# Eight groups' second product in plain float32, their weights split a block a slot later, and four units' row remainder on TensorE

## The chip, the cores and the metric

The kernel runs on one core of a Trainium2 chip. Its engines work side by side, each in its own order: TensorE (PE in the rows; PEld is its weight load), VectorE (DVE), ScalarE (ACT), GpSimd (POOL) and SyncE (SP), which issues the transfers. The metric is the device time in microseconds of one execution; lower is better.

## The reference

Three stages follow each other. The change touches the first two.

```python
for t in range(S):                        # S = 768, 4 batches, 8 heads of width 48
    cur = einsum('bhd,bhe->bhde', u * kt, vt)
    y[:, :, t] = einsum('bhd,bhde->bhe', rt, state + cur)
    state = wt[..., None] * state + einsum('bhd,bhe->bhde', kt, vt)
# x = y with the heads side by side: [4, 768, 384]
h = maximum(x @ w_in, 0)                  # w_in [384, 1024], float64
gate = 1 / (1 + exp(-conv3(h, conv_w)))   # three taps along the sequence
x2 = (h * gate) @ w_out                   # w_out [1024, 384], float64
# then causal attention with 4 experts of width 64, two chosen per row
```

The scan's inputs are float32; w_in, conv_w and w_out come as float64 and are made float32 on the chip.

## The kernel before

**Units and groups.** The scan is cut into 32 units u: a batch, a half of the sequence (384 steps) and a pair of heads. Units 0 to 3 are the four pairs of the first half of batch 0, units 4 to 7 of its second half, and so on. The middle stage is cut into 64 groups g = 8 bh + f: bh is a half of a batch, f one of eight blocks of 128 columns of w_in. A group is a product `hs` (`mlp1`, L434, nine matmuls), ReLU on ScalarE into `ht`, three taps (`conv_a`, `conv_b`, into `ct`), tanh (L471, into `st`) and the gate (`gate`, L480), and then the second product `x` with w_out (`mlp2`, L508), which adds over the eight f of a bh into three PSUM tiles.

**Three products for one.** A float32 matrix is held as a high part rounded to fp32r and a low part, the rest. A product takes high x high, low x high and high x low. For `x` that is nine matmuls a group: `high` (L487, ScalarE) and `low` (L495, VectorE) make the two parts of the gated rows, and the parts of w_out stand in two tiles `wout0` and `wout1`. The rows of the scan get their two parts in `rows`: ScalarE copies the rounded rows out of PSUM (L408), VectorE subtracts (L409), and two to four transfers bring both into X, the input of `hs` (L417).

**Weights.** `load_w` brings a block of w_in or w_out, four each, as float64. `conv0_w` and `conv1_w` make float32 of it by work on the bits (VectorE, ScalarE, GpSimd), `conv2_w` rounds it to the high part (L209, ScalarE), `conv3_w` subtracts (L214, VectorE). The table `WS` says in which slot a block begins; its conv2 and conv3 are one slot later, for w_out in slots 5, 7, 8 and 9.

**The order.** For TensorE, VectorE, ScalarE and GpSimd the order is the code's own: `slot(u)` is written out by hand, and each engine does its instructions in that order, waiting where an input or a buffer is not there. SyncE's order is the scheduler's. With ga = 2u - 11, slot u holds `hs` of groups ga and ga + 1, each followed by `x` of three groups earlier: group 0 is begun in slot 5, `x` of group 0 in slot 7, of group 7 in slot 10. Around them, on TensorE: `trans(u)` (L325), `es` for the early units (L330), `hs`, `x`, `scores` (L310), `state` (L343), `yout(u - 1)` (L388, L396), from slot 8 on `carried` (L359), `hs`, `x`. On VectorE: taps of the group before, `scan_d(u + 1)` (L249), `queries`, `gate`, `low`, `scan_f` (L257), taps, `keys` (L264), `low`, `gate`, the weights' conv3 and conv1, `masked` (L316), the row part of unit u - 1 (L409), from slot 8 on `carry2` (L372). On ScalarE the copies and tanh of the same steps, `scaled` (L353, `Ss`) among them; `trans` of the next slot needs the PSUM buffer that `scaled` reads. From slot 8 on, `carry2` sends the state through two transfers into Bd, which `yout` of the next slot reads.

Of the kernel before, what the change touches and what calls it, by code (L numbers as in the profile page):

```python
# [10 lines left out]
F32 = mybir.dt.float32  # L11
# [5 lines left out]
OP = mybir.AluOpType  # L17
# [33 lines left out]
def _f(ap):  # L51
    return ap.bitcast(F32)
# [52 lines left out]
def phase1(tc, nc, a, x2, ident, stat, lim, top, right, left2):  # L105
# [83 lines left out]
    win = [wt.tile([128, 4, 3, 256], F32R, name=f"win{i}") for i in range(2)]  # L189
    wout = [wt.tile([128, NF, DM], F32R, name=f"wout{i}") for i in range(2)]  # L190
    both = dict(win=win, wout=wout)
    wl = lambda t: t.rearrange("p a b c -> p (a b c)") if len(t.shape) == 4 else t.rearrange("p a b -> p (a b)")
# [9 lines left out]
    def conv1_w(n, i):  # L202

        if wide:
            RW[n, i] = f64_fast(nc, raw, RW[n, i], RW.pop((n, i, 0)), WC, "w")

    def conv2_w(n, i):

        nc.scalar.activation(wl(both[n][0])[:, i * WC:(i + 1) * WC], RW[n, i], AF.Copy)  # L209

    def conv3_w(n, i):
        t = RW.pop((n, i))
        d0, d1 = (wl(d)[:, i * WC:(i + 1) * WC] for d in both[n])
        nc.vector.tensor_tensor(d1, t, _f(d0), op=OP.subtract)  # L214

# [184 lines left out]
    def rows(u):  # L400
# [73 lines left out]
    def gate(g):  # L474
        if not 0 <= g < NG:
            return
        h = g // NF % 2
        o, N = 2 * h, HT - 2 + 4 * h
        ht, st = G[g]
        nc.vector.scalar_tensor_tensor(st, st, 1.0, ht[:, o:o + N], op0=OP.add, op1=OP.mult)  # L480
        G[g] = st

    def high(g):
        if not 0 <= g < NG:
            return
        gh = ml.tile([128, HT + 2], F32R, name="gh", bufs=LAG + 2)[:, 0:HT - 2 + 4 * (g // NF % 2)]
        nc.scalar.activation(gh, G[g], AF.Copy)  # L487
        G[g] = gh, G[g]

    def low(g):  # L490
        if not 0 <= g < NG:
# [8 lines left out]
    def mlp2(g):  # L500
# [3 lines left out]
        if f == 0:  # L504
            acc[0] = [ps_x.tile([128, HT + 2], F32, name=f"x{i}") for i in range(3)]
        for i in range(3):
            for z, (wi, gi) in enumerate(((0, 0), (1, 0), (0, 1))):
                nc.tensor.matmul(acc[0][i][:, 0:N], wout[wi][:, f, i * 128:(i + 1) * 128], G[g][gi],  # L508
                                 start=(f == 0 and z == 0), stop=(f == NF - 1 and z == 2))
# [25 lines left out]
    def slot(u):  # L535
# [741 lines left out]
```

## Time and profile before

| | us |
|---|---|
| median of 3 runs | 610.92 (610.88 to 611.37) |
| the profiled execution | 614.61 |
| its span, first to last instruction | 612.9 |
| TensorE busy in the span | 573.2 (94%) |
| VectorE busy | 493.8 (81%) |
| ScalarE busy | 400.0 (65%) |

Busy times of engines overlap, so they don't add up to the span. A busy share is a mean over stages of different limits; what a change in one stage is worth is read in that stage. Matmuls are pipelined: a matmul's own length is longer than its distance from the next, so their pace is read from start to start. A bracket at the end of a row in order of time gives the engine's idle time ahead of the row and who ended it. [...]

### The profile page before, as it was taken

The numbers are of one execution on the slowest core, as the hardware profiler recorded it, in microseconds if no ns is written. First come the engines' busy times: TensorE is split into PE (matmuls) and PEld (weight loads), VectorE is DVE, ScalarE is ACT, GpSimd is POOL, SyncE is SP. The second block draws the span as 40 slices with busy tenths as digits, with TensorE's granted clock in tenths as the row PEclk, the third lists the DMA queues.
The fourth block names the chain that finished last, engine by engine and source line by source line (L and its number), as shares of the span: only waits on it lengthen the run. The fifth ranks groups of instructions, "written<-read, shape, count | busy, mean of one in ns | idle before, by whom it ended". The sixth has DMA issues, their size and how long they took to land.

```text
span 612.9 us, 12380 instructions
## 1 busy us (share of the span) xinstructions
PE 573.2 (94%) x4374; PEld 514.4 (84%) x4374; DVE 493.8 (81%) x1139; ACT 400.0 (65%) x1013; POOL 188.6 (31%) x246
## 2 busy tenths in 40 slices
PE   4998988999999999999997999999979998999896
PEld 4887877999989999899997999797869887888754
DVE  6999999999999999999866955996748683876561
ACT  4886656777767888897765755865556555656542
POOL 3665563434524344242416300300030002004070
PEclk9999889999999999999999999999998999899999
DMA  8886445655656668776235425661265226422502
GB/s 283 279 268 186 144 137 139 184 144 143 206 159 184 180 218 297 216 219 164 73 83 160 141 52 151 172 156 40 65 180 136 60 78 167 111 67 72 141 2 83
DMA packets 46583, 91.00 MB, mean 148 GB/s; under 512 B 14256, under 2 KB 27824, under 8 KB 46512
## 3 DMA queue, kind: packets, MB, share of 16 engines
q1 hardware_dynamic: 46512, 90.12, 50.8%
q8 instruction: 37, 0.61, 0.4%
q14 instruction: 34, 0.28, 0.1%
HBM read 50.82 MB, written 9.44 MB: 98 GB/s over the span
## 4 chain that ended last, share of the span: by engine, by line
PE 59%; DVE 19%; ACT 8%; DMA 6%; issue 3%; POOL 2%; SPq 1%; ACTq 0%; DVEq 0%; POOLq 0%
PE hs L434 11%; PE x L508 10%; PE m L925 8%; PE st L999 6%; PE m L1049 6%; PE t L1033 5%; PE m L1061 4%; PE m L955 4%; DMA x<-x 3%; DVE Dp L249 3%; PE sc L310 2%; DVE ct L453 2%; DVE Fp L257 2%; PE m L396 2%; DVE ct L466 2%
## 5 line engine op out<-in xcount | busy, mean ns | idle before, releaser
L434 PE MATMUL hs<-X,win 128*128 128x384 f32 (+1 forms) x576 | 120.7, 355 | 4.5 <-ACT ht L438 4.4
L434 PEld LDWEIGHTS hs<-X,win 128*128 128x128 f32 x576 | 101.0, 193 | 8.1 <-ACT ht L438 5.8
L508 PE MATMUL x<-gh,wout 128*128 128x386 f32 (+1 forms) x384 | 99.2, 340 | 0.0
L293 POOL TENSOR_SCALAR_AFFINE_SELECT AT<-e 128x384 f32<-128x384 f32 x52 | 44.1, 869 | 125.3 <-DVE e L283 102.0
L1013 ACT ACTIVATE A<-sm,mn 128x128 f32<-128x128 f32 (+5 forms) x96 | 63.7, 664 | 23.2 <-DVE mn L1012 22.5
L1012 DVE CUSTOM_DVE_ANT_0 sm<-st,mask 128x128 f32<-128x128 f32 (+5 forms) x96 | 58.1, 616 | 20.5 <-PE st L999 19.0
L471 ACT ACTIVATE st<-ct 128x382 f32<-128x382 f32 (+1 forms) x64 | 33.6, 526 | 62.4 <-DVE ct L466 34.4
L508 PEld LDWEIGHTS x<-gh,wout 128*128 128x128 f32 x384 | 71.0, 191 | 0.0
L508 PE MATMUL x<-gl,wout 128*128 128x382 f32 (+1 forms) x192 | 65.3, 340 | 0.0
L1033 PE MATMUL t<-ident,A 128*128 128x128 f32 x336 | 53.2, 276 | 2.2 <-ACT T L1037 1.3
L911 POOL TENSOR_TENSOR xs<-x,xs 128x768 fp32r<-128x768 f32 x12 | 22.5, 1887 | 85.4 <-ACT xs L910 85.4
L1033 PEld LDWEIGHTS t<-ident,A 128*128 128x128 f32 x336 | 40.2, 141 | 9.8 <-ACT T L1037 2.2
L1039 DVE COPY T<-t 128x128 f32<-128x128 f32 (+3 forms) x64 | 32.2, 504 | 19.5 <-PE t L1033 18.9
L999 PE MATMUL st<-sk,sq 128*128 128x384 f32 (+3 forms) x128 | 45.5, 368 | 1.4 <-DVE mn L1012 1.1
L1037 ACT ACTIVATE T<-t 128x512 f32<-128x512 f32 (+3 forms) x64 | 28.5, 446 | 26.3 <-PE t L1033 21.6
L999 PE MATMUL st<-sl,sq 128*128 128x384 f32 (+3 forms) x128 | 41.8, 340 | 4.0 <-DMA sl<-kl 4.0
L480 DVE SCALAR_TENSOR_TENSOR st<-st,ht 128x382 f32<-128x382 f32 (+1 forms) x64 | 37.0, 578 | 9.4 <-ACT st L471 7.5
L1049 PE MATMUL m<-T,V 128*64 128x384 f32 (+2 forms) x288 | 43.1, 421 | 0.0
L438 ACT ACTIVATE ht<-hs 128x384 f32<-128x384 f32 (+1 forms) x64 | 31.1, 485 | 16.4 <-PE hs L434 16.3
L442 ACT ACTIVATE ct<-ht,cwk 128x382 f32<-128x382 f32 (+1 forms) x64 | 39.5, 617 | 2.0
L495 DVE TENSOR_TENSOR gl<-st,gh 128x382 fp32r<-128x382 f32 (+1 forms) x64 | 38.6, 602 | 2.1 <-ACT gh L487 1.9
L249 DVE TENSOR_TENSOR_SCAN Dp<-wkr,cD 128x387 f32<-128x387 f32 x32 | 36.7, 1145 | 4.2 <-POOL cD L165 4.0
(146 smaller groups left out, 1344.9 us busy)
## 6 DMA issues: line engine op xcount, KB each, us to landing
wkr<-in_wkr SPq DMA_DIRECT2D x31, 578.0 KB, 4.3
rn<-in_rkv SPq DMA_DIRECT2D x22, 288.0 KB, 3.2
v<-in_rkv SPq DMA_DIRECT2D x32, 192.0 KB, 3.6
rawt<-in_win SPq DMA_DIRECT2D x8, 768.0 KB, 7.2
rawt<-in_wout SPq DMA_DIRECT2D x8, 768.0 KB, 5.2
sk<-kh SPq DMA_DIRECT2D x32, 192.0 KB, 3.3
sl<-kl SPq DMA_DIRECT2D x32, 192.0 KB, 4.0
x<-x SPq DMA_DIRECT2D x12, 384.0 KB, 3.9
```

Of the source, the lines that this page charges most:

```text
L249: nc.vector.tensor_tensor_scan(fl(t["Dp"]), t["w"][:, 0:NW], fl(cD), 0.0, op0=OP.mult, op1=OP.add)
L293: nc.gpsimd.affine_select(AT[:, j], t["e"][:, j][:, :, None].to_broadcast([128, CH, C]), pattern=[[0, CH], [1, C]], compare_op=OP.is_equal ...
L434: nc.tensor.matmul(hs[:, 0:N], win[wi][:, f // 2, i, (f % 2) * 128:(f % 2 + 1) * 128], x[:, i, xi], start=(n == 0), stop=(n == 8))
L442: nc.scalar.activation(ct, ht[:, o:o + N], AF.Copy, scale=w[:, 1, f:f + 1])
L495: nc.vector.tensor_tensor(gl, gt, _f(gh), op=OP.subtract)
L508: nc.tensor.matmul(acc[0][i][:, 0:N], wout[wi][:, f, i * 128:(i + 1) * 128], G[g][gi], start=(f == 0 and z == 0), stop=(f == NF - 1 and z ...
L925: nc.tensor.matmul(pt[:, 0:HT], w[wi][:, i, p * 128:(p + 1) * 128], xs[xi][:, i, s], start=(m == 0), stop=(m == 8))
L999: nc.tensor.matmul(st[:, z, 0:n], q[:, qi * C:(qi + 1) * C], k[:, z * n:(z + 1) * n], start=(i == 0), stop=(i == 1))
L1012: nc.vector.tensor_tensor_reduce(o3, i3, m3, 1.0, 3e38, op0=OP.add, op1=OP.min, accum_out=mn)
L1013: nc.scalar.activation(at, o3, AF.Exp, bias=mn, scale=-1.0, accum_out=rs[:, qi % 3:qi % 3 + 1])
L1033: nc.tensor.transpose(pt[:, ki - k0], at[:, ki * C:(ki + 1) * C], self.ident)
L1049: nc.tensor.matmul(po[o, lo:HT], V[:, ki, (2 * p + j) * 64:(2 * p + j + 1) * 64], Ts[j][:, ki, lo:], start=(ki == 0), stop=(ki == n - 1))
```

## The change

- `x` of groups 0 to 7 (`PLAIN = 8`): three plain float32 matmuls a group instead of nine fp32r ones. Their weights are w_out in plain float32 (`wpl`, four tiles, which GpSimd's last step of conv1 writes directly); `gate` writes the rows into a float32 tile, and `high` and `low` are left out for these groups.
- The parts of w_out for groups 8 and on are made later, one block a slot: `split1_w` (ScalarE, high part, at the end of slots 8 to 11), `split2_w` (VectorE, slots 9 to 12, ahead of `masked`), `split3_w` (ScalarE, slots 10 to 13, rounds the low part into the place of the plain block).
- Rows of units 4 to 7 (`LOW_ON_PE`): the low part is made a slot later by TensorE, which adds `minus` (the negative identity) times the rounded rows to the rows in PSUM; ScalarE copies the result. The transfers into X go out after that, at the start of the next slot (`rows_out`).

```diff
+LOW_ON_PE = range(4, 8)
+PLAIN = 8
+SPLIT = 8
...
-    wout = [wt.tile([128, NF, DM], F32R, name=f"wout{i}") for i in range(2)]
+    wout = wt.tile([128, NF, DM], F32R, name="wout0")
+    wpl = [wt.tile([128, 2, DM], F32, name=f"wout1{i}") for i in range(4)]
+    wlo = {}
...
+    def split1_w(i):
+        nc.scalar.activation(wl(wout)[:, i * WC:(i + 1) * WC], wl(wpl[i]), AF.Copy)
+
+    def split2_w(i):
+        t = RW["lo", i] = raw.tile([128, WC], F32, name="wm")
+        nc.vector.tensor_tensor(t, wl(wpl[i]), wl(_f(wout))[:, i * WC:(i + 1) * WC], op=OP.subtract)
+
+    def split3_w(i):
+        wlo[i] = wt.tile([128, 2, DM], F32R, name=f"wout1{i}")
+        nc.scalar.activation(wl(wlo[i]), RW.pop(("lo", i)), AF.Copy)
...
-        nc.vector.tensor_tensor(Y[:, 1, 4 * h:], yf, _f(Y[:, 0, 4 * h:]), op=OP.subtract)
+        T[u]["Y"] = Y
+        if u not in LOW_ON_PE:
+            nc.vector.tensor_tensor(Y[:, 1, 4 * h:], yf, _f(Y[:, 0, 4 * h:]), op=OP.subtract)
+
+    def rows_low(u):
...
+        nc.tensor.matmul(yf, minus, Y[:, 0, 4 * h:], start=False, stop=True, skip_group_check=True)
+        nc.scalar.activation(Y[:, 1, 4 * h:], yf, AF.Copy)
...
+        if g < PLAIN:
+            gt = ml.tile([128, HT + 2], F32, name="gh", bufs=LAG + 2)[:, 0:N]
+            nc.vector.scalar_tensor_tensor(gt, st, 1.0, ht[:, o:o + N], op0=OP.add, op1=OP.mult)
+            G[g] = gt
+            return
...
         for i in range(3):
+            if g < PLAIN:
+                nc.tensor.matmul(acc[0][i][:, 0:N], wpl[f // 2][:, f % 2, i * 128:(i + 1) * 128], G[g], start=(f == 0),
+                                 stop=(f == NF - 1))
+                continue
...
         if s1u:
             trans(u)
+        if u - 2 in LOW_ON_PE:
+            rows_low(u - 2)
+            rows_out(u - 2)
+        if 0 <= u - SPLIT - 2 < 4:
+            split3_w(u - SPLIT - 2)
...
+            if n == "wout" and u == SPLIT + 1 + m:
+                split2_w(m)
...
+        for m in range(4):
+            if u == SPLIT + m:
+                split1_w(m)
```

TensorE in slot 7, from the last `hs` of group 3 on (`x_859` to `x_861` are the three PSUM tiles). Before:

```order
L434 MATMUL hs<-X,win_148 128x384
L508 MATMUL x_859<-gh,wout_149 128x382
L508 MATMUL x_859<-gh,wout_150 128x382
L508 MATMUL x_859<-gl,wout_149 128x382
L508 MATMUL x_860<-gh,wout_149 128x382
L508 MATMUL x_860<-gh,wout_150 128x382
L508 MATMUL x_860<-gl,wout_149 128x382
L508 MATMUL x_861<-gh,wout_149 128x382
L508 MATMUL x_861<-gh,wout_150 128x382
L508 MATMUL x_861<-gl,wout_149 128x382
L310 MATMUL sc<-Q,K 128x128 x6
```

Now:

```order
L471 MATMUL hs<-X,win_150 128x384
L550 MATMUL x_858<-gh,wout_152 128x382
L550 MATMUL x_859<-gh,wout_152 128x382
L550 MATMUL x_860<-gh,wout_152 128x382
L334 MATMUL sc<-Q,K 128x128 x6
```

Nine fp32r products became three plain ones, of which each runs as two records in a trace. At the start of the same slot the product with `minus` (`m<-Y,minus`) now stands between `es` and the first `hs`.

VectorE in the second half of slot 7, from the last tap on. Before:

```order
L466 SCALAR_TENSOR_TENSOR ct<-ht,cwk,ct 128x382
L280 TENSOR_TENSOR wkr<-wkr 128x384
L495 TENSOR_TENSOR gl<-st,gh 128x382
L480 SCALAR_TENSOR_TENSOR st<-st,ht 128x382
L214 TENSOR_TENSOR wout_150<-wm,wout_149 128x768
L93 SCALAR_TENSOR_TENSOR wm<-rawt,wm 128x768
L316 COPY_PREDICATED AT<-msk,sc 128x384 x2
L409 TENSOR_TENSOR Y<-m,Y 128x384
```

Now:

```order
L503 SCALAR_TENSOR_TENSOR ct<-ht,cwk,ct 128x382
L304 TENSOR_TENSOR wkr<-wkr 128x384
L519 SCALAR_TENSOR_TENSOR gh<-st,ht 128x382
L96 SCALAR_TENSOR_TENSOR wm<-rawt,wm 128x768
L340 COPY_PREDICATED AT<-msk,sc 128x384 x2
```

The low part of the gated rows, of the weights and of the scan's rows are gone; all three stood behind the taps.

VectorE at the end of slot 10 (`Ss` is `carry2`, behind which Bd is sent). Before:

```order
L283 TENSOR_REDUCE e<-rn 128x6
L495 TENSOR_TENSOR gl<-st,gh 128x386
L480 SCALAR_TENSOR_TENSOR st<-st,ht 128x386
L316 COPY_PREDICATED AT<-msk,sc 128x384 x2
L409 TENSOR_TENSOR Y<-m,Y 128x384
L372 SCALAR_TENSOR_TENSOR Ss_129<-Ss_129,Dp 128x48
```

Now:

```order
L307 TENSOR_REDUCE e<-rn 128x6
L537 TENSOR_TENSOR gl<-st,gh 128x386
L522 SCALAR_TENSOR_TENSOR st<-st,ht 128x386
L234 TENSOR_TENSOR wm<-wout_153,wout_151 128x768
L340 COPY_PREDICATED AT<-msk,sc 128x384 x2
L435 TENSOR_TENSOR Y<-m,Y 128x384
L396 SCALAR_TENSOR_TENSOR Ss_131<-Ss_131,Dp 128x48
```

A weight block's low part now stands ahead of `masked` and of `carry2` here, as it does in slots 9 to 12.

## Rows read from the trace of the kernel before

**Rows 1.** The page's span in 40 slices: busy tenths, and granted TensorE clock.

```profile
DVE  6999999999999999999866955996748683876561
...
PEclk9999889999999999999999999999998999899999
```

**Rows 2.** Busy time by stretch: start:end, length, engines' busy (instructions), clock, transfers.

```profile
64.70:76.79 12.09, 11.70 (x99) 10.89 (x98) 12.02 (x22) 7.92 (x19) 6.25 (x10) 1.00 0.51 160
76.79:90.15 13.36, 10.46 (x92) 9.30 (x91) 13.29 (x22) 7.96 (x20) 8.82 (x13) 0.94 0.32 100
...
111.38:121.01 9.63, 9.63 (x89) 9.17 (x89) 9.33 (x19) 7.89 (x22) 3.70 (x6) 1.00 0.69 212
```

The engines of Rows 2 stand in the order PE, PEld, DVE, ACT, POOL.

**Rows 3.** TensorE in order of time: start, length, line, count, [idle ahead].

```profile
60.23 0.44 PE L325 MATMUL m<-ident,K 128*128 128x128 f32 x2 [1.87 <-ACT Ss L353]
...
61.79 3.18 PE L434 MATMUL hs<-X,win 128*128 128x384 f32 x9 [0.56 <-ACT ht L438]
...
69.19 1.84 PE L434 MATMUL hs<-X,win 128*128 128x384 f32 x9
70.87 0.51 PE L508 MATMUL x<-gh,wout 128*128 128x382 f32 x2
...
72.42 0.49 PE L325 MATMUL m<-ident,K 128*128 128x128 f32 x3
...
73.86 1.84 PE L434 MATMUL hs<-X,win 128*128 128x384 f32 x9 [0.39 <-ACT ht L438]
...
81.81 0.32 PE L359 MATMUL m<-Ss,ident 128*64 128x48 f32 x4 [1.72 <-ACT Ss L353]
...
86.67 0.55 PE L325 MATMUL m<-ident,K 128*128 128x128 f32 x3 [1.19 <-ACT Ss L353]
...
87.64 2.39 PE L434 MATMUL hs<-X,win 128*128 128x384 f32 x9
89.83 0.84 PE L508 MATMUL x<-gh,wout 128*128 128x382 f32 x2
...
92.52 0.94 PE L310 MATMUL sc<-Q,K 64*128 64x128 f32 x12
...
96.46 0.54 PE L396 MATMUL m<-Q,Bd 128*64 128x128 f32 x5 [1.54 <-DMA Bd<-Ss]
...
100.42 0.49 PE L325 MATMUL m<-ident,K 128*128 128x128 f32 x3
...
106.71 0.73 PE L396 MATMUL m<-Q,Bd 128*64 128x128 f32 x7 [0.61 <-DMA Bd<-Ss]
```

**Rows 4.** ScalarE's waits for the taps, 60 to 101 us (total, times, longest); one earlier.

```profile
ACT st L471 <- DVE ct L466: 14.2, 6, 3.5
...
59.27 0.52 ACT L471 ACTIVATE st<-ct 128x382 f32<-128x382 f32 x1 [0.49 <-DVE ct L466]
```

**Rows 5.** Groups by line and shape: count, busy us, mean ns of one, idle before.

```profile
L508 PEld LDWEIGHTS x<-gh,wout 128*128 128x128 f32 x384 | 71.0, 191 | 0.0
...
L495 DVE TENSOR_TENSOR gl<-st,gh 128x382 fp32r<-128x382 f32 x32 | 18.4, 576 | 1.5 <-ACT gh L487 1.3
...
L409 DVE TENSOR_TENSOR Y<-m,Y 128x384 fp32r<-128x384 f32 x32 | 17.4, 542 | 0.7 <-ACT Y L408 0.7
...
L214 DVE TENSOR_TENSOR wout<-wm,wout 128x768 fp32r<-128x768 f32 x4 | 3.8, 946 | 0.0
```

**Rows 6.** Plain float32 products in order of time: attention's `av`, and `es`.

```profile
413.50 3.45 PE L1049 MATMUL m<-T,V 128*64 128x384 f32 x24
...
60.50 0.73 PE L330 MATMUL m<-u_c,wkr 128*128 128x2 f32 x6
```

**Rows 7.** SyncE's issues in order of time; median time to landing of such a transfer.

```profile
90.53 2.46 SPq L417 DMA_DIRECT2D X<-Y  x4
...
102.62 1.34 SPq L377 DMA_DIRECT2D Bd<-Ss  x2
...
X<-Y SPq DMA_DIRECT2D x8, 97.0 KB, 2.2
```

More of the change, by code (lines that the diff above doesn't have):

```diff
@@ L173, in phase1 @@
     nc.vector.tensor_copy(msk, ones3)
+    minus = cst.tile([128, 128], F32R, name="minus")
+    nc.scalar.activation(minus, ident, AF.Copy, scale=-1.0)
     Ss = []
@@ L189, in phase1 @@
     win = [wt.tile([128, 4, 3, 256], F32R, name=f"win{i}") for i in range(2)]
-    wout = [wt.tile([128, NF, DM], F32R, name=f"wout{i}") for i in range(2)]
-    both = dict(win=win, wout=wout)
+    wout = wt.tile([128, NF, DM], F32R, name="wout0")
+    wpl = [wt.tile([128, 2, DM], F32, name=f"wout1{i}") for i in range(4)]
+    wlo = {}
     wl = lambda t: t.rearrange("p a b c -> p (a b c)") if len(t.shape) == 4 else t.rearrange("p a b -> p (a b)")
@@ L204, in conv1_w @@
         if wide:
-            RW[n, i] = f64_fast(nc, raw, RW[n, i], RW.pop((n, i, 0)), WC, "w")
+            RW[n, i] = f64_fast(nc, raw, RW[n, i], RW.pop((n, i, 0)), WC, "w",
+                                wl(wpl[i]) if n == "wout" else None)
     def conv2_w(n, i):
-        nc.scalar.activation(wl(both[n][0])[:, i * WC:(i + 1) * WC], RW[n, i], AF.Copy)
+        t = RW[n, i]
+        if n == "wout":
+            if not wide:
+                nc.scalar.activation(wl(wpl[i]), t, AF.Copy)
+            return
+        nc.scalar.activation(wl(win[0])[:, i * WC:(i + 1) * WC], t, AF.Copy)
     def conv3_w(n, i):
         t = RW.pop((n, i))
-        d0, d1 = (wl(d)[:, i * WC:(i + 1) * WC] for d in both[n])
-        nc.vector.tensor_tensor(d1, t, _f(d0), op=OP.subtract)
+        if n == "win":
+            d0, d1 = (wl(d)[:, i * WC:(i + 1) * WC] for d in win)
+            nc.vector.tensor_tensor(d1, t, _f(d0), op=OP.subtract)
+    def split1_w(i):
[6 more added lines that the diff above has]
+        nc.scalar.activation(wl(wlo[i]), RW.pop(("lo", i)), AF.Copy)
     RW = {}
@@ L408, in rows, with rows_out @@
         nc.scalar.activation(Y[:, 0, 4 * h:], yf, AF.Copy)
-        nc.vector.tensor_tensor(Y[:, 1, 4 * h:], yf, _f(Y[:, 0, 4 * h:]), op=OP.subtract)
+        T[u]["Y"] = Y
+        if u not in LOW_ON_PE:
+            nc.vector.tensor_tensor(Y[:, 1, 4 * h:], yf, _f(Y[:, 0, 4 * h:]), op=OP.subtract)
+    def rows_low(u):
+        b, h, hp = split(u)
+        Y = T[u]["Y"]
+        yf = T[u]["y"].rearrange("p c t -> p (c t)")
+        nc.tensor.matmul(yf, minus, Y[:, 0, 4 * h:], start=False, stop=True, skip_group_check=True)
+        nc.scalar.activation(Y[:, 1, 4 * h:], yf, AF.Copy)
+    def rows_out(u):
+        b, h, hp = split(u)
+        Y = T[u]["Y"]
         if not h:
@@ L479, in gate @@
         ht, st = G[g]
+        if g < PLAIN:
+            gt = ml.tile([128, HT + 2], F32, name="gh", bufs=LAG + 2)[:, 0:N]
+            nc.vector.scalar_tensor_tensor(gt, st, 1.0, ht[:, o:o + N], op0=OP.add, op1=OP.mult)
+            G[g] = gt
+            return
         nc.vector.scalar_tensor_tensor(st, st, 1.0, ht[:, o:o + N], op0=OP.add, op1=OP.mult)
@@ L483, in high @@
     def high(g):
-        if not 0 <= g < NG:
+        if not PLAIN <= g < NG:
             return
@@ L490, in low @@
     def low(g):
-        if not 0 <= g < NG:
+        if not PLAIN <= g < NG:
             return
@@ L506, in mlp2 @@
         for i in range(3):
+            if g < PLAIN:
+                nc.tensor.matmul(acc[0][i][:, 0:N], wpl[f // 2][:, f % 2, i * 128:(i + 1) * 128], G[g], start=(f == 0),
+                                 stop=(f == NF - 1))
+                continue
             for z, (wi, gi) in enumerate(((0, 0), (1, 0), (0, 1))):
-                nc.tensor.matmul(acc[0][i][:, 0:N], wout[wi][:, f, i * 128:(i + 1) * 128], G[g][gi],
+                w = wlo[f // 2][:, f % 2] if wi else wout[:, f]
+                nc.tensor.matmul(acc[0][i][:, 0:N], w[:, i * 128:(i + 1) * 128], G[g][gi],
                                  start=(f == 0 and z == 0), stop=(f == NF - 1 and z == 2))
@@ L607, in slot @@
             rows(u - 1)
+            if u - 1 not in LOW_ON_PE:
+                rows_out(u - 1)
         if CARRY_ON_PE <= u < 2 * NU:
```

## The prediction, on record before the result was known

> **What bounds the kernel now.** I first read the page's slices [rows 1]. VectorE stands at 9 from the second slice to the nineteenth, up to about 290 us, and the granted clock falls to 8 in two of them only, 61 to 92 us. So something there differs from the later slots. The table of busy time by stretch [rows 2] says what: its stretches are slots 7, 8 and 11, cut where VectorE starts `scan_d`. In slots 7 and 8 VectorE is busy 12.02 of 12.09 and 13.29 of 13.36 us. In slot 11 a slot takes 9.63 us and TensorE is the full engine. The early slots are thus up to 3.7 us longer than the later ones, and VectorE sets them.
>
> Then I read TensorE's order of time [rows 3] for what that costs there. Its slots start at `trans` (L325): 60.23, 72.42, 86.67 and 100.42 us, so slots 7 to 9 take 12.19, 14.25 and 13.75. Idle in them: 0.56 and 0.39 us for `ht`, 1.72 and 1.19 us for `Ss` on ScalarE, and 1.54 us for the transfer into Bd; in slot 10 0.61 us for Bd again. ScalarE itself is no cause: in this stretch its tanh waits 14.2 us in six times for `ct` of VectorE [rows 4], and `Ss` and `ht` stand behind the tanh on the same engine. Bd is sent only when VectorE's `carry2` (L372) has run. So all these waits except the first lead back to VectorE's late work.
>
> The clock is a second loss. Nine matmuls `hs` take 1.68 us from 69.19 to 70.87, and nine `x` 1.55 us from 70.87 to 72.42. [...]
>
> **The change part by part.** *VectorE loses work.* Each `low` of the first eight groups was 0.58 us, each low part of a row 0.54, each `wout` low part 0.95 [rows 5]. Slots 7 and 8 lose two `low`, one row part and one weight part each: 2 x 0.58 + 0.54 + 0.95 = 2.65 us. Slot 6 loses 1.1, slot 9 two `low` (1.16; its weight part is replaced by a new one). That leaves 9.4 us in slot 7 and 10.6 in slot 8, less than TensorE will need there. Slot 5 loses 1.5 us, which I count at nothing: the `ct` that begins slot 6 waits for the first `hs`, whose start the removed work does not touch.
>
> The waits that end: 0.39 + 1.72 + 1.19 + 1.54 + 0.61 = 5.45 us, and with the 1.19 the slow stretch of 1.65: **7.1 us**. I leave the 0.56, the 1.87 us before 60.23 and the slow `hs` from 61.79 (3.18 us where the one from 69.19 has 1.84): the idle before 60.23 hangs on the tanh at 59.27, which waits for `ct` [rows 4], and in slot 6 all that is removed from VectorE stands behind that `ct`.
>
> *TensorE gains work.* The trace of before has no full-width plain product of this size. The nearest is attention's `av` [rows 6]: 24 matmul records in 3.45 us, two column halves beside each other, so twelve in a row. A plain product is two records; a half here has eight of 384, two of 256 and two of 128 columns, 3840 in all. Without the last one's tail (its length less its turn, about 0.17 us) that is 3.28 / 3840 = 0.85 ns a column; for 382 columns 0.33 us a record, 1.96 us for the six of a group. Nine fp32r ones took 1.55. So +0.41 a group, **+3.3 us** for eight. [...] For the upper end, the weights are 128 columns wide here and 64 there. In `es` [rows 6] six records of two columns with 128-wide weights take 0.73 us, at most 0.12 us each, all of it load. Were none of that hidden, 48 records would add 5.8 us more. I take it as hidden, since `x` already loads 128-wide weights beside shorter matmuls.
>
> [...]
>
> The four products with `minus` are fp32r of 384 columns, 1.68 / 9 = 0.19 us each. They stand between `trans` and the slot's first `hs`. In slots 6 and 7 TensorE waits for `ht` or has room there; in slots 8 and 9 they count, **+0.4 us**. In slot 9 they are followed by four transfers into X, which used to go out at the end of slot 8.
>
> *ScalarE* loses eight `high` and four weight copies and gains four row copies and eight weight copies, twelve for twelve; but the weight copies now stand at the end of slots 8 to 11 and the start of slots 10 to 13. Its waiting (14.2 us in this stretch) is the cover, so I count nothing; behind the new copies stand `ht` and the tanh, for which TensorE and VectorE would wait if that cover is gone.
>
> *The weights' low part comes back on VectorE* in slots 9 to 12, 0.95 us each, ahead of `masked` and L372. In slot 11 VectorE was busy 9.33 of 9.63 [rows 2], and slot 12 has the same work; 10.28 is 0.65 too much each time, 1.3 in all. Bd is behind it: the transfers of slot 9 were issued from 102.62 [rows 7], and TensorE got them at 106.71 after 0.61 of waiting. That is the wait which may return in slots 11 to 13. VectorE then starts with some lead, so I charge about half, **0.6 us**.
>
> Sum: 7.1 - 3.3 - 0.4 - 0.6 = 2.8 us. Profiled execution: 614.61 - 2.8 = 611.8; the median of the runs lies 3.69 lower, 610.92 - 2.8 = **608.1 us**. Everything behind slot 13 moves as a block, since TensorE is the full engine there. Where a half-clock stretch of the attention stage falls may move with it, by something like the 1.65 us of one such stretch, either way.
>
> **The rivals.** (a) *The late split takes the gain back.* VectorE is over its slot in 11 and 12, the row parts are still there, and Bd makes TensorE wait in three slots. For it: a single weight part in slot 9 went with 0.61 us of wait in slot 10, and four such waits are 2.4 us. Against it: in slots 9 and 10 two and one `low` are gone. Price: 1.8 us beyond my 0.6; 609.9 us.
>
> (b) *Slower: the plain products' weight loads are not hidden.* Plain loads come in twice the number per product, and no row shows 128-wide plain loads under a long matmul. Price 48 x 0.12 = 5.8 us, so 613.9. It decides from 4.0 us on (more than 0.083 us a record), where the change is a loss beyond 0.2%. For it speaks `es`; against it that `x` hides its loads under matmuls half as long.
>
> (c) *The new rows come too late.* The X transfers of unit 7 now go out after `trans(9)` and a ScalarE copy. Before, four were issued in 2.46 us from 90.53 [rows 7], and the `hs` that reads them began only after the Bd wait that ended at 96.46. After, TensorE reaches that `hs` some 7 to 8 us after `trans(9)` (9.79 before, from 86.67 to 96.46, less the 1.54 and 1.65, plus the plain group and the row product); `es` 0.73, product, copy, four issues of 2.46 and 2.2 us of landing are about 6.5. Price 0 to 1 us: inside the forecast's range. (d) *More:* the waits of slots 6 and 7 (1.87 and 0.56) and the slow part of that `hs` (1.34) go too, and no split cost: 2.8 + 0.6 + up to 3.8, so 603.7 to 606. That needs VectorE to be earlier before 59 us, which the order speaks against.
>
> [...] (f) It doesn't do what it says: TensorE is not relieved because ScalarE, which now has the row copy between `trans` and the tanh, holds `Ss` back by such a copy, about 0.5 us (the tanh of the same width takes 0.52 [rows 4]), in four slots. Then 2 us go: 610.1.
>
> **How the numbers follow.** Two medians of this kernel can be told apart from about 0.2%, 1.2 us, on; so faster is below 609.7 and slower above 612.1. Forecast with (c): 0.58, from 606.3 to 609.6. (a) 0.13 and (f) 0.05, mostly within 0.2%. (b) 0.10, slower. (d) 0.09 and (e) 0.02, faster. The rest, 0.03, I put on a small gain or loss in the noise of half-clock stretches. Faster 0.58 + 0.09 + 0.02 + a share of (a) and (f), 0.03 = 0.72; slower 0.10; the same 0.18. The range reaches from 605.0, which takes half of (d), to 611.3, which takes (a) and (f): what is left out is (b), (e), the rest of (d) and little else, under 0.2.
>
> **What would show it.** In the profile of the changed kernel: a group's six plain records of `x` take 1.9 to 2.0 us (right), or 2.5 and more (b); VectorE has idle time in slots 7 and 8; TensorE's waits for `Ss` and Bd in slots 8 to 10 are gone or below 0.3 us, and no half clock near 88 us; slots 7 to 9 sum to about 36.5 us instead of 40.2; slot 6 is still as long on TensorE. If Bd waits stand in slots 11 to 13, the late split costs what (a) says. If idle time in slots 8 and 9 stays though VectorE has room, I was wrong on who ends those waits.

## The result, and the profile after

The changed kernel is slower: 616.35 us median (612.62 to 619.25) against 611.55 (609.79 to 618.00) for the kernel before, 22 runs each; ratio 1.0065, 95% interval 1.0042 to 1.0087. A ratio here compares all runs of the two kernels and is not the quotient of the two medians. The forecast was 608.1, in a range from 605.0 to 611.3. The profiled execution took 618.18 us with a span of 616.5.

The page's slices of the changed kernel (busy tenths of VectorE, granted TensorE clock in tenths of full speed), to lay beside [rows 1]:

```profile
DVE  6999997999999999999866756896748774875461
...
PEclk9869998999999999999999999999999999899898
```

VectorE has a gap in the seventh slice (92 to 108 us). That is later than forecast: in slots 7 and 8 it is busy 12.98 of 13.10 and 11.13 of 11.45 us, in slot 10 7.80 of 10.12. The clock is below 9 in six slices, in four before. Of the late ones, the 35th (524 to 539 us) is low in both kernels. The 38th (570 to 586 us) is low in the changed kernel alone, and there the change does not touch a single instruction. The second and third (15 to 46 us) can't be compared. The page shows full clock there for the kernel before, yet its first `hs` of slot 5 takes 3.11 us, the changed kernel's 1.84 (start, length, line, count; before, then changed):

```profile
48.30 3.11 PE L434 MATMUL hs<-X,win 128*128 128x384 f32 x9
...
48.08 1.84 PE L471 MATMUL hs<-X,win 128*128 128x384 f32 x9
```

The same kernel by stretch (start:end, length, busy us of PE, PEld, DVE, ACT, POOL, clock, transfers; slots 8, 9 and 12, cut at TensorE's `trans`):

```profile
71.88:83.33 11.45, 11.45 (x93) 9.03 (x92) 11.13 (x17) 6.41 (x17) 8.57 (x12) 1.00 0.38 113
83.33:98.22 14.89, 12.69 (x89) 9.78 (x88) 13.05 (x23) 8.61 (x23) 7.04 (x9) 0.89 0.65 176
...
117.78:128.97 11.19, 9.76 (x88) 9.05 (x86) 11.13 (x22) 7.83 (x20) 6.07 (x8) 1.00 0.55 151
```

TensorE's order of time in the changed kernel (start, length, line, count, [idle ahead]), for [rows 3]:

```profile
69.96 2.09 PE L550 MATMUL x<-gh,wout 128*128 128x382 f32 x6
71.88 0.49 PE L349 MATMUL m<-ident,K 128*128 128x128 f32 x3
...
92.94 2.07 PE L471 MATMUL hs<-X,win 128*128 128x388 f32 x9 [2.20 <-DMA X<-Y]
94.80 3.59 PE L550 MATMUL x<-gh,wout 128*128 128x382 f32 x6
98.22 0.49 PE L349 MATMUL m<-ident,K 128*128 128x128 f32 x3
...
125.00 0.54 PE L420 MATMUL m<-Q,Bd 128*64 128x128 f32 x5 [1.43 <-DMA Bd<-Ss]
```

Slot 8 now takes 11.45 us instead of 14.25, with TensorE full, and the waits for `Ss` and Bd of slots 8 to 10 are gone. Slot 9 is 14.89 us long (13.75 before): TensorE waits 2.20 us for the rows in X, and the products behind that wait run at half clock: the granted clock is 0.50 from 94.41 to 97.82, and six records take 3.42 us (94.80 to 98.22) instead of 1.92. Slot 12 has a new wait for Bd, 1.43 us, and is 11.19 us instead of 9.35. Slot 7 is 0.91 us longer (13.10), slot 5 1.50 us shorter (9.58 instead of 11.08), 1.27 of it in the `hs` above. By slot 13 (129.66 before, 128.97 after) 0.7 us of the gain is left, and at the last `trans` 0.4 (302.93 and 302.57). So this execution lost its time after 303 us: 310.0 us remain there before, 313.9 after.

Two of TensorE's waits in the attention stage, first of the kernel before:

```profile
515.79 0.48 PE L999 MATMUL st<-sl,sq 128*128 128x256 f32 x2 [1.10 <-DMA sl<-kl]
520.18 0.62 PE L925 MATMUL m<-xs,wq 128*128 128x384 f32 x2 [1.52 <-ACT xs L910]
...
575.56 0.65 PE L999 MATMUL st<-sl,sq 128*128 128x512 f32 x2 [1.56 <-DMA sl<-kl]
```

and of the changed one:

```profile
520.62 0.64 PE L984 MATMUL m<-xs,wq 128*128 128x384 f32 x2 [2.30 <-ACT xs L969]
...
577.58 0.65 PE L1058 MATMUL st<-sl,sq 128*128 128x512 f32 x2 [2.31 <-DMA sl<-kl]
```

The last one is 0.75 us longer for the same transfers of the same data. Why was the question of the experiments.

### The profile page after: what moved, and what is told of

Same layout as the page of the kernel before. It is cut to its first block, busy times and chain, and to the rows that moved or that the text cites. A ratio compares the mean times of both kernels' runs of the same rounds, so it can differ in the third digit from the quotient of the medians.

```text
span 616.5 us, 12329 instructions
## 1 busy us (share of the span) xinstructions
PE 572.7 (93%) x4354; PEld 507.1 (82%) x4354; DVE 491.1 (80%) x1127; ACT 401.0 (65%) x1014; POOL 188.7 (31%) x246
## 4 chain that ended last, share of the span: by engine, by line
PE 55%; DVE 20%; ACT 9%; DMA 9%; issue 3%; POOL 2%; SPq 1%; ACTq 0%; DVEq 0%; POOLq 0%
PE hs L471 9%; PE m L984 7%; PE x L555 7%; PE st L1058 6%; PE m L1108 6%; PE t L1092 5%; PE m L1120 4%; PE m L1014 4%; DVE Dp L273 3%; DMA x<-x 3%; DVE Fp L281 2%; PE x L550 2%; PE sc L334 2%; DMA wkr<-in_wkr 2%; DVE ct L490 2%
## 5 line engine op out<-in xcount | busy, mean ns | idle before, releaser
L471 PE MATMUL hs<-X,win 128*128 128x384 f32 (+1 forms) x576 | 119.1, 351 | 5.8 <-ACT ht L475 3.6
L555 PE MATMUL x<-gh,wout 128*128 128x386 f32 (+1 forms) x336 | 87.1, 341 | 0.0
L555 PEld LDWEIGHTS x<-gh,wout 128*128 128x128 f32 x336 | 62.2, 191 | 0.0
L555 PE MATMUL x<-gl,wout 128*128 128x386 f32 (+1 forms) x168 | 57.3, 341 | 0.0
L522 DVE SCALAR_TENSOR_TENSOR st<-st,ht 128x386 f32<-128x386 f32 (+1 forms) x56 | 32.8, 585 | 10.9 <-ACT st L508 9.3
L325 ACT ACTIVATE Fp<-wkr,lim 128x384 f32<-128x384 f32 x64 | 38.8, 606 | 0.3
```

Of the source, the lines that this page charges most:

```text
L325: nc.scalar.activation(Fp[:, :, 0:C], wc, AF.Relu, bias=lim[:, z:z + 1], scale=(-1.0, 1.0)[z], accum_out=stat[:, 2 * u + z:2 * u + z + 1])
L471: nc.tensor.matmul(hs[:, 0:N], win[wi][:, f // 2, i, (f % 2) * 128:(f % 2 + 1) * 128], x[:, i, xi], start=(n == 0), stop=(n == 8))
L555: nc.tensor.matmul(acc[0][i][:, 0:N], w[:, i * 128:(i + 1) * 128], G[g][gi], start=(f == 0 and z == 0), stop=(f == NF - 1 and z == 2))
```

## Experiments: the parts

Theory 1 was that the X rows of unit 7 come too late, theory 2 that the late split of the weights takes the gain back, theory 3 that the medians differ by where half-clock stretches of the attention stage fall. Four edits, each timed against the kernel before (612.65 us median, 608.69 to 616.45).

**Rows alone.** The kernel before with `LOW_ON_PE`, `rows_low` and `rows_out`, without the plain products.

```diff
+LOW_ON_PE = range(4, 8)
...
+        if u - 2 in LOW_ON_PE:
+            rows_low(u - 2)
+            rows_out(u - 2)
```

> The kernel before with one part of the change: units 4 to 7 get their rows' low part from TensorE a slot later; the second product and the weights are as before. Theory 1 (the loss of the first stage is made by transfers: X of unit 7 leaves a slot later and lands late, in the changed kernel 2.20 us of idle at slot 9 and a stretch of half clock behind it): this kernel shows a wait for X in slot 9, and slot 13 begins 0 to 2 us later than before (129.66). Theory 2 (the changed kernel's loss lies in its plain products or late weights, not in the rows): no X wait, slot 13 within 0.5 us of 129.66 or earlier. On the whole time, theory 3 (half-clock stretches of the attention stage fall by chance and carry most of the difference of the medians): the whole time differs from before by more than slot 13 does, either way.

Measured: 613.55 us, ratio 1.0025 (1.0002 to 1.0048). There is no wait for X in slot 9; TensorE waits 1.61 us for Bd there, as it did before (1.54). Slot 13 begins at 128.25, 1.4 us earlier than before and not later, and slot 5 alone is 1.5 us shorter. So this edit does not test theory 1: TensorE waits for Bd first, as before.

**Plain products alone.**

```diff
-LOW_ON_PE = range(4, 8)
+LOW_ON_PE = ()
```

> The changed kernel without its rows part: VectorE makes all low parts of rows as before, X goes out at the end of each slot; plain products and late weights stay. Theory 1 (X): the X wait of 2.20 us and the slow stretch behind it (1.9 us) in slot 9 are gone, 4 x 0.54 us of VectorE come back; slot 13 begins near 126 to 128 (changed kernel 128.97, before 129.66), the median falls by 1 to 3 us from the changed kernel's 616.35. Theory 2 (plain products or late weights): slot 13 stays at 129 or later. Theory 3 (chance in the attention stage): the median stays at 614 to 617 though slot 13 is early.

Measured: 614.12 us, 1.0012 (0.9984 to 1.0040), 2.2 us below the changed kernel's 616.35. The wait for X is gone, but TensorE waits 1.81 us for Bd in slot 9 and 1.23 in slot 12, and slot 13 begins at 128.29, between what theories 1 and 2 said.

**Unit 7 back on VectorE.**

```diff
-LOW_ON_PE = range(4, 8)
+LOW_ON_PE = range(4, 7)
```

> The changed kernel with the rows part for units 4 to 6 alone, so that X of unit 7, the last that group 8 needs, goes out at the end of slot 8 again. Theory 1: no X wait in slot 9, no half clock there, slot 10 begins near 94 to 95 (changed kernel 98.22), slot 13 near 126 to 127. Theory 2: slot 13 at 129 as in the changed kernel, because VectorE's late weight parts take it back by Bd. Theory 3: the median stays above 614 whatever slot 13 does.

Measured: 614.57 us, 1.0035 (1.0009 to 1.0061). The wait for X and the half clock behind it are gone, slot 9 takes 12.37 us instead of 14.89. TensorE there (the `hs` follows without idle):

```profile
91.44 0.54 PE L420 MATMUL m<-Q,Bd 128*64 128x128 f32 x5 [1.17 <-DMA Bd<-Ss]
92.12 1.86 PE L471 MATMUL hs<-X,win 128*128 128x388 f32 x9
93.82 2.08 PE L550 MATMUL x<-gh,wout 128*128 128x382 f32 x6
```

Theory 1 is thus shown for slot 9, but a wait of 1.17 us for Bd stands in its place: SyncE now issues the X transfers (85.41) between the two of Bd (84.60 and 87.92). A second profile of the changed kernel, taken later, prices the wait for X without half clock behind it:

```profile
92.53 1.86 PE L471 MATMUL hs<-X,win 128*128 128x388 f32 x9 [1.74 <-DMA X<-Y]
```

Slot 9 takes 12.76 us there, only 0.4 more than with unit 7 back; the other 2.1 us of 14.89 go with the half clock. At the last `trans` the kernel with unit 7 back is 2.4 us ahead of before (300.57), and its median is behind it. Its gain is lost later, too.

**The split's subtraction on GpSimd** (beside the edit above).

```diff
-        nc.vector.tensor_tensor(t, wl(wpl[i]), wl(_f(wout))[:, i * WC:(i + 1) * WC], op=OP.subtract)
+        nc.gpsimd.tensor_tensor(t, wl(wpl[i]), wl(_f(wout))[:, i * WC:(i + 1) * WC], op=OP.subtract)
```

> As the kernel with unit 7 back, and the four late low parts of the weights (0.95 us each on VectorE) on GpSimd, which is idle for two thirds of slots 9 to 12. If the Bd wait of slot 12 (1.43 us in the changed kernel) is made by VectorE's late weight parts, it is gone here and slot 13 begins 1 to 2 us earlier than in the kernel with unit 7 back; if Bd is late for another reason (transfers beside it), the wait stays. Theory 3: the median stays above 614 whatever slot 13 does.

Measured: 616.32 us, 1.0041 (1.0015 to 1.0067). Slot 12 stays at 10.71 us and slot 13 grows to 11.22. The wait for Bd in slot 12 is gone, but TensorE waits 1.17 and 1.41 us for `Ss` of ScalarE in slots 12 and 13: the subtraction takes 2.2 to 2.5 us on GpSimd, and ScalarE's rounding copy, with `Ss` behind it, waits 2.00 and 3.33 us for it. So moving it to GpSimd is no cure, and the edit does not show what the split costs on VectorE.

## Experiments: the first stage by itself

To see in which stage the medians differ, four kernels were cut after the first stage. They leave out attention and write the first stage's result.

```diff
-    at.open_right()
-    at.run()
-    at.right.close()
+    for b in range(B):
+        nc.sync.dma_start(out[b].rearrange("(p s) d -> p (s d)", p=128), x2[:, b].rearrange("p o t -> p (o t)"))
```

> The kernel before without its attention stage: the output is the first stage's result copied out, the attention products, softmax and output projection are left out. It is the base for the next three. By the profile of before the last transposed unit begins at 302.9 us and the first stage's last products are done near 345 us, so some 350 us. Theory A (the changed kernel loses its time in the attention stage, by where half-clock stretches of TensorE fall there) and theory B (it loses it in the first stage, and the one profiled execution of before was a poor sample of that stage) say nothing different of this one; its spread over 12 runs shows how much of the spread of the whole kernel (608.7 to 616.5) belongs to the first stage: A wants under 2 us, B 4 us or more.

> The changed kernel, cut in the same way. Theory A: the two profiles agree to 0.4 us at the last unit (302.93 and 302.57), so 0 to -1 us against the base. Theory B: the whole difference of the medians is made here, +3 to +5 us against the base.

> The changed kernel with unit 7's low rows back on VectorE (units 4 to 6 on TensorE), cut in the same way. Theory A: as its profile, -2.4 us against the base. Theory B: +1 to +2.5 us against the base, as the medians of the whole kernels.

> The changed kernel with all low rows on VectorE (plain products and late weights alone), cut in the same way. Theory A: as its profile, -0.4 us against the base. Theory B: +1 to +1.5 us against the base.

| cut after the first stage, 5 runs each | median us | lowest to highest | against before |
|---|---|---|---|
| before | 376.64 | 375.82 to 378.47 | |
| changed | 375.71 | 371.05 to 379.03 | -0.9 |
| unit 7 back | 374.49 | 373.02 to 375.84 | -2.2 |
| plain products alone | 373.22 | 372.67 to 374.82 | -3.4 |

Cut, two of the three gain; the changed kernel's 0.9 us lies within the spread of its own five runs (8 us). Plain products alone gain 3.4 us, where theory A had 0.4. Whole, none is ahead, though plain products alone can't be told from before. So most of the loss arises behind the first stage, as theory 3 says; but being in the medians of 12 and 22 runs, it is not chance alone. The attention stage has the same instructions in both traces, and its operations last as long as before (the 16 exponentials of 768 columns 935 ns in both). What differs is how many instructions stand ahead of it: before has 4374 matmul records and 1139 VectorE instructions, the changed kernel 4354 and 1127. The page's first lines, before and changed:

```profile
PE 573.2 (94%) x4374; PEld 514.4 (84%) x4374; DVE 493.8 (81%) x1139; ACT 400.0 (65%) x1013; POOL 188.6 (31%) x246
...
PE 572.7 (93%) x4354; PEld 507.1 (82%) x4354; DVE 491.1 (80%) x1127; ACT 401.0 (65%) x1014; POOL 188.7 (31%) x246
```

The trace of the transfers has packets of a kind "instruction" over the whole span: 37 of 16 KB on queue 8 and 34 of 8 KB on queue 14 before, 36 and 34 in the changed kernel. Queue 8 has 37 in each of three pages with 4374 matmul records (before, changed padded on both, plain alone padded) and 36 in both with 4354 (the changed kernel twice). Theory C takes these packets for the engines' reads of their own instructions: with fewer instructions ahead, a later read falls at another place of the attention stage, and that is the loss. In the changed kernel one such read, of queue 14, lies at 573 us, among the four `sl` transfers for which TensorE waits 2.31 us; in the kernel before, none does. Three more reads of that queue, at 560 to 562 us, stay where they were; which engine's they are was not shown.

## Experiments: the same instructions, read at other places

**Padding.** 10 tiny float32 matmuls and 13 tiny copies on VectorE at the start of the kernel give both engines their number of instructions back (4374 and 1140). They write scratch, or a value that is already there.

```diff
+    pt = ps_m.tile([128, 512], F32, name="m")
+    for _ in range(10):
+        nc.tensor.matmul(pt[:, 0:2], ident, ident[:, 0:2], start=True, stop=True)
...
     nc.vector.tensor_copy(msk, ones3)
+    for _ in range(13):
+        nc.vector.tensor_copy(msk[:, 0, 0:1], ones3[:, 0, 0:1])
```

> The changed kernel with 10 float32 matmuls of 2 columns and 13 copies of one column on VectorE at its start, where both engines wait for data; they write scratch or repeat a value. They give TensorE and VectorE back the number of instructions that the change took from them (before: 4374 matmul records and 1139 VectorE instructions in the profile, after: 4354 and 1127). Theory C (the instructions of the second stage are the same, but their reads from memory fall at other places, since these go by the number of instructions before; one read beside the sl transfers makes TensorE wait 2.31 instead of 1.56 us near 577 us and its clock halves): the read of queue 14 is back near 561, the wait is 1.5 to 1.6 us, and the median is 2 to 5 us below that of the changed kernel in the same comparison. Theory D (chance where half-clock stretches fall): no change, within 1 us.

> The changed kernel with the 13 copies on VectorE alone. Theory C: the read of queue 14 and the wait near 577 go back as with both (1.5 to 1.6 us), TensorE's own reads (queue 8) stay where they are in the changed kernel; the median between the changed kernel and the one with both, 1.5 to 3 us below the changed one. Theory D: within 1 us of the changed kernel.

> The changed kernel unedited, as the base of the other three, and for a second trace. Ratio to before 1.004 to 1.009 if its loss is real, under 1.003 if it was chance. In its trace: X wait in slot 9 (2 us) and Bd wait in slot 12 (1.4 us) again, if they belong to the order of work and not to one execution; the wait for sl near 577 at 2.3 us again by theory C, anything from 1.5 to 2.5 by theory D.

> Unit 7's low rows back on VectorE, and the padding on both engines (13 copies are one more than this version lacks). Cut after the first stage this version gained 2.2 us against before, whole it lost 2.1. Theory C: the first stage's gain is kept, 1 to 3 us below before. Theory D: as without the padding, 1 to 3 us above before.

Then, to tell the place of the reads from the padding as such (but for the `LOW_ON_PE` of the third, the `for` counts alone differ):

> The kernel before with the same padding (10 small matmuls, 13 copies on VectorE). Theory C: VectorE's read of before at 562 us moves some 10 us ahead, to about 551, away from the sl transfers as before; wait for sl near 575 stays 1.5 to 1.6 us, median within 1.5 us of before. Theory E (the padding helps in itself, for instance by what TensorE does in its first microseconds): 3 to 5 us below before, as it did for the changed kernel.

> The changed kernel with the 10 small matmuls alone. Theory C: VectorE's read stays near 570 us, the wait for sl near 575 stays 2.3 us with half clock behind it in most executions; the median 613 to 615.5, above the kernel with both paddings (610.67) by 2 us or more. Theory E with TensorE as the cause: as with both, 610 to 611.

> The changed kernel with all low rows on VectorE, so the plain products and the late weights alone, with 12 small matmuls and 8 copies, which restore the counts of before. Without padding it stood at 1.0012 of before. Its VectorE read was at 561 already and its wait for sl 1.57, but a read at 522 lay beside the wait for xs at 520 (2.46 us in one piece, half clock behind it; before 1.10 and 1.52 in two). Theory C: that read goes back to 509 to 514, the wait is in two pieces, median 609.5 to 612. Theory E for TensorE or VectorE: 609 to 611 too; chance: as without, 613 to 614.

> The changed kernel with 10 small matmuls and 6 copies in place of 13. Theory C: VectorE's read falls half way between 570 and 560, near 565, some 3 us ahead of the four sl transfers, so the wait for sl is 1.5 to 1.6 us and the median 610 to 612. If the number of instructions matters and not the place of the read: between 610.7 and 614.

Measured, 12 runs each, against before at 612.67 us (changed again, padded on both, VectorE padded, unit 7 back) and 612.77 us (the other four); "read" says whether an instruction read of queue 14 lies among the four `sl` transfers ahead of that place, "half" whether a half-clock stretch follows there in the profiled execution:

| kernel | median us | ratio (95%) | near 515: read, waits for sl + xs, half | near 575: read, wait for sl, half |
|---|---|---|---|---|
| before | 612.67 and 612.77 | | yes, 1.10 + 1.52, yes | no, 1.56, no |
| changed, again | 615.66 | 1.0047 (1.0019 to 1.0074) | no, 0.38 + 2.40, yes | yes, 2.33, yes |
| changed, padded on both | 610.67 | 0.9974 (0.9953 to 0.9995) | yes, 0.97 + 1.82, no | no, 1.55, no |
| changed, VectorE padded | 613.48 | 0.9998 (0.9974 to 1.0022) | yes, 1.06 + 1.61, no | no, 1.54, no |
| changed, TensorE padded | 613.93 | 1.0015 (0.9986 to 1.0044) | no, 0.36 + 2.25, yes | yes, 2.35, yes |
| changed, TensorE and 6 copies | 613.11 | 0.9998 (0.9971 to 1.0026) | no, 0.38 + 2.20, yes | no, 1.55, no |
| unit 7 back, padded | 610.50 | 0.9966 (0.9944 to 0.9989) | yes, 1.01 + 1.71, no | no, 1.57, no |
| plain alone, padded | 610.30 | 0.9954 (0.9926 to 0.9982) | yes, 1.11 + 1.70, yes | no, 1.53, no |
| before, padded | 616.78 | 1.0055 (1.0021 to 1.0089) | no, 0.39 + 2.13, yes | no, 1.56, no |

Twenty-three useless instructions take 5 us off the changed kernel, and the same ones make the kernel before 4.0 us slower (3.5 without its two slowest runs). So it is not the padding as such, and theory E is refuted. Theory C's expectation for that run held for the wait near 575 (1.56 us) but not for the median, which it had within 1.5 us of before: what the padding costs there arises in the first stage, and theory C does not explain it (last section). For the attention stage of the changed kernel theory C stands. The rows that carry it are the transfers in 6 us around the four `sl` (queue and kind: packets, MB, share; then the `sl` issues: count, KB each, median us to landing). The changed kernel again, 568 to 574 us:

```profile
q14 instruction: 1, 0.01, 0.4%
...
sl<-kl SPq DMA_DIRECT2D x4, 192.0 KB, 4.5
```

The padded one at the same place, 565 to 571 us; there is no instruction read in it:

```profile
q1 hardware_dynamic: 567, 1.40, 98.6%
sl<-kl SPq DMA_DIRECT2D x4, 192.0 KB, 3.9
```

One packet of 8 KB among 560 lies beside transfers that land 0.6 us later, in a stretch in which the transfer engines are 97 to 99% busy. How so short a read delays all four the traces don't show. At the other place it is the reverse. The padded kernel, 506 to 512 us:

```profile
q14 instruction: 1, 0.01, 0.3%
sl<-kl SPq DMA_DIRECT2D x4, 192.0 KB, 4.4
```

and the changed kernel again, 507 to 513:

```profile
q1 hardware_dynamic: 563, 1.39, 98.2%
sl<-kl SPq DMA_DIRECT2D x4, 192.0 KB, 4.0
```

Here a read costs nothing: TensorE waits for `xs` next in any case, and the two waits come to 0.97 + 1.82 = 2.79 us with the read and 0.38 + 2.40 = 2.78 without. TensorE of the padded kernel:

```profile
512.44 0.47 PE L1063 MATMUL st<-sl,sq 128*128 128x256 f32 x2 [0.97 <-DMA sl<-kl]
...
517.12 0.61 PE L989 MATMUL m<-xs,wq 128*128 128x384 f32 x2 [1.82 <-ACT xs L974]
...
571.05 0.65 PE L1063 MATMUL st<-sl,sq 128*128 128x512 f32 x2 [1.55 <-DMA sl<-kl]
```

and of the changed kernel again:

```profile
512.69 0.48 PE L1058 MATMUL st<-sl,sq 128*128 128x256 f32 x2 [0.38 <-DMA sl<-kl]
...
517.97 1.01 PE L984 MATMUL m<-xs,wq 128*128 128x384 f32 x2 [2.40 <-ACT xs L969]
...
574.65 0.65 PE L1058 MATMUL st<-sl,sq 128*128 128x512 f32 x2 [2.33 <-DMA sl<-kl]
```

The two `wq` products behind the wait take 0.61 us in the one and 1.01 in the other: after the longer piece of idle time half clock follows (the granted clock is 0.87 from 505 to 531 us, and 1.00 from 505 to 530 in the padded kernel). What that costs is in the busy time from the `xs` wait to the `sl` wait, and from there to the end; the padded kernel first:

```profile
517.12:571.05 53.93, 51.31 (x349) 44.30 (x349) 37.53 (x126) 31.76 (x81) 9.19 (x7) 1.00 0.40 101
571.05:608.20 37.15, 30.14 (x183) 21.59 (x183) 17.86 (x50) 16.67 (x43) 10.79 (x12) 0.97 0.15 49
```

the changed kernel again:

```profile
517.97:574.65 56.68, 54.16 (x349) 46.82 (x350) 37.70 (x126) 31.83 (x81) 9.19 (x7) 0.94 0.39 99
574.65:614.50 39.85, 31.69 (x183) 22.48 (x183) 17.85 (x50) 16.67 (x43) 10.79 (x12) 0.90 0.12 42
```

The same 349 and 183 matmuls: 56.68 - 53.93 = 2.75 us and 39.85 - 37.15 = 2.70 us. In the first 0.78 is the longer wait for `sl`; the other 2.0 us are what the half clock leaves after a wait for VectorE has shrunk by 0.9 behind it. In the second only 1.55 us are clock (TensorE busy 31.69 instead of 30.14). The other 1.15 stand behind the last matmul (6.67 us to the end instead of 5.52), in this execution alone: in the other 13 profiles the end comes 5.5 to 5.8 us after it. So the two places explain 2.75 + 1.55 = 4.3 of the 6.3 us between the two spans; the medians are 4.99 apart.

Over all 14 profiles of whole kernels (these nine, the four of the first section and the changed one's first) the pattern holds. Near 575 the wait is 2.28 to 2.35 us in five of them (the changed kernel twice, unit 7 back, split on GpSimd, TensorE padded), each with a read of queue 14 among the `sl`, and 1.53 to 1.57 in the nine others. Half clock follows in four of the five and in none of the nine. From the end of that wait to the last matmul the four take 33.15 to 33.18 us, the ten others 31.61 to 31.64. So the read near 575 costs 0.78 us of waiting, and 1.55 us more where half clock follows. Near 515, an undivided wait for `xs` of 2.1 to 2.5 us was followed by half clock in nine profiles out of nine; a divided one in two out of five.

Which engine's read it is follows from the two halves of the padding. VectorE's 13 copies alone take the read of queue 14 away from the `sl` near 575; TensorE's 10 matmuls alone do not:

```profile
573.44 0.65 PE L1061 MATMUL st<-sl,sq 128*128 128x512 f32 x2 [2.35 <-DMA sl<-kl]
```

The kernel with 6 copies lies between the two. One read has moved away, the other has not yet moved in, and the median is in between:

```profile
518.16 0.61 PE L989 MATMUL m<-xs,wq 128*128 128x384 f32 x2 [2.20 <-ACT xs L974]
...
573.66 0.65 PE L1063 MATMUL st<-sl,sq 128*128 128x512 f32 x2 [1.55 <-DMA sl<-kl]
```

Its median missed the expectation (610 to 612), which had left out the first place. Against the kernel with TensorE's padding alone (613.93) it is 0.8 us lower, which is within the noise: the price of the read near 575 by itself comes from profiles, not from medians.

A read need not hold TensorE up: in slot 10 of the changed kernel, with a read of queue 8 at 106.9 us (one packet, 0.02 MB), TensorE is busy 10.12 of 10.12 us. Near 575 the read goes with a cost to another engine: TensorE waits for the `sl` transfers 2.28 to 2.35 us with it and 1.53 to 1.57 without.

## Why the prediction was wrong, step by step

*The waits that end (7.1 us).* Right as to what they hang on: `Ss` and Bd are no longer waited for in slots 8 to 10, and the half clock near 88 us is gone (the granted clock was 0.50 from 88.66 to 92.07 before). Its 1.65 us are in [rows 3]: from 87.64 nine `hs` take 2.19 us and nine `x` 2.69, from 69.19 they take 1.68 and 1.55. The sign that was named for it did not show, since VectorE stays busy in slots 7 and 8 and has its idle time in slots 9 and 10. But slot 9's 1.54 us and its slow clock came back under another name, as rival (c). Its price, 0 to 1 us, was mis-sized: TensorE waits 2.20 us, and half clock follows in that execution (1.74 us and none in the second). Of the sum of about 6.5 us two terms were short. SyncE of the changed kernel:

```profile
84.64 1.41 SPq L401 DMA_DIRECT2D Bd<-Ss  x2
86.14 0.55 SPq L135 DMA_DIRECT2D wkr<-in_wkr  x1
86.79 2.47 SPq L454 DMA_DIRECT2D X<-Y  x4
```

The X transfers are queued behind two of Bd and a load of 578 KB, and land 3.7 us after the last issue (89.26 to 92.94), where the sum had the median of 2.2 [rows 7]. With unit 7 back on VectorE the wait is gone, and 1.17 us of waiting for Bd come back.

*The plain products (+3.3 us).* Right: 1.92 us for six records (69.96 to 71.88), forecast 1.96. Rival (b), weight loads that show, is refuted by the same row: the six loads take 1.65 us beside these matmuls (69.78 to 71.43). In the kernel before the loads of `x` lie beside its matmuls, too: one lasts 191 ns [rows 5], and nine matmuls follow each other in 1.55 us, 0.172 us each. Rival (e), a time below the forecast's range, did not come: a group's product takes 0.37 us more than before (1.92 for 1.55), with six loads in place of nine. Rival (d) did not come: the wait for `Ss` ahead of slot 7 is 1.75 us (1.87 before). Nor did rival (f) in the slots that it named: no wait for `Ss` is left in slots 8 and 9.

*The late split (+0.6 us).* Too small. TensorE reaches slot 12 2.5 us earlier, VectorE's `carry2` is only 0.6 us earlier (118.87, 119.49 before), and Bd makes TensorE wait 1.43 us. VectorE of the changed kernel, the split's subtraction ahead of it:

```profile
116.58 0.95 DVE L234 TENSOR_TENSOR wm<-wout,wout 128x768 f32<-128x768 f32 x1
...
118.87 0.36 DVE L396 SCALAR_TENSOR_TENSOR Ss<-Ss,Dp 128x48 f32<-128x48 f32 x1
```

That is rival (a) in kind, and its price (2.4 us with the 0.6) was nearer than the 0.6: slots 12 and 13 together take 1.7 to 1.8 us more than before (20.6 to 20.8 for 18.9) in the changed kernel and the padded one alike (in the latter TensorE waits for `Ss` of ScalarE instead, 0.79 and 0.46 us). Slot 17 takes 0.8 to 1.0 us more for Bd in every profile with the late split but the changed kernel's first; yet the padded kernel before, which has no late split, waits for Bd there too, so that part can't be put down to it.

*The sum (2.8 us).* For the first stage it was of the right size, in part by luck. At the last `trans` the two profiles of the changed kernel are 0.4 and 1.9 us ahead of before, with unit 7 back 2.4; cut, the gains are 0.9, 2.2 (unit 7 back) and 3.4 us (plain products alone). For slots 7 to 10 (50.63 us before) the terms give 47.2, and the two profiles show 49.56 and 47.47. In the second, slot 9 is 1.2 us longer than its terms say and slots 8 and 10 0.5 each shorter. Slot 5, counted at nothing, gave 1.5 us, most of it in its first `hs` (3.11 and 1.84 us). That can't be credited to the change: with one and the same work the slot takes 11.19 us (plain products alone) or 9.57 (the same, padded). With the instruction counts put back, the whole kernel gains 2.0 us (612.67 to 610.67), or 2.5 with the plain products alone.

*"Everything behind slot 13 moves as a block".* This is the step that failed. It allowed for half-clock stretches that move by chance, ±1.65 us, and missed what moves them for good: the number of instructions ahead, with which the reads moved (of queue 14 one from 560 to 573 us, with 12 instructions fewer on VectorE). That term was +5 us by the medians (615.66 against 610.67; two places in the profiles account for 4.3 of it), larger than all others but the first, and it turned a gain of 2 into a loss of 3 to 5. None of the rivals named it, and the one on the slower side (b) was another mechanism. The page of before already had these reads in two rows of its third part (queue and kind: packets, MB, share), on which the prediction spent no thought:

```profile
q8 instruction: 37, 0.61, 0.4%
q14 instruction: 34, 0.28, 0.1%
```

## What to carry to other kernels

When an edit removes or adds instructions on an engine, ask which tight transfers of later stages its instruction reads will then fall on; a stage that is identical can still change by several microseconds (here 4.3 us in two places), and padding the count back with a few idle instructions separates this from the edit's own effect. Here the best version is the plain products alone, with the counts restored (610.30 us, 0.9954 of before), and the rows' part adds nothing that can be told from it. The count is not neutral for a tuned kernel either: the kernel before lost about 4 us to the same 23 instructions, in the first stage and for a reason that was not found.

## What was not expected of the hardware, and what stays open

- One instruction read of 8 KB among some 1.4 MB of transfers went with a wait of TensorE of 2.33 instead of 1.55 us, in five profiles of five with it and none of nine without, and with the half clock that followed in four of them cost 2.3 us in one place.
- Idle time of the same sum, 2.8 us, was followed by half clock in one piece (0.38 + 2.40) and not in two (0.97 + 1.82). Over all profiles it is nine of nine in one piece and two of five in two; what decides it was not shown.
- Open: the reads of queue 8. With VectorE's padding alone the median is 2.8 us above that of both. In its profile a read of queue 8 lies at 390 us, and TensorE waits 1.15 us for `sl` there, which the kernel padded on both does not (it is also 3.8 us later at the last `trans`, 304.47 for 300.71, which no read of the attention stage explains):

```profile
392.84 0.35 PE L1060 MATMUL st<-sl,sq 128*128 128x256 f32 x1 [1.15 <-DMA sl<-kl]
```

That is one profile, and a part of the difference at best. TensorE's padding alone lowers the median by 1.7 us (613.93) though the read near 575 stays; why was not found.

- Open: how the padded kernel before loses some 4 us. At the last `trans` it is already 4.05 us behind (306.98), with longer waits for Bd in slots 9 and 17, the first followed by half clock; what delays those transfers was not traced.

```profile
97.90 0.54 PE L401 MATMUL m<-Q,Bd 128*64 128x128 f32 x5 [1.35 <-DMA Bd<-Ss]
...
178.12 0.54 PE L401 MATMUL m<-Q,Bd 128*64 128x128 f32 x5 [1.58 <-DMA Bd<-Ss]
```

- Open: after a wait for `ht` of 1.94 to 1.99 us near 335, half clock follows in ten of the eleven profiles with the plain products and in none of the three without them (before, rows alone, before padded), though the wait is the same. It costs the former some 1.6 us; why was not found.
